# Two pairs' products with v in one TensorE run, token units of 256 and 320, and more pairs with v stationary, in a fused attention and two-MLP kernel

## The chip, the core and the metric

The kernel runs on one core of one Trainium2 chip. The metric is the device time of one execution in microseconds, lower is better. TensorE (PE) does the matrix products, VectorE (DVE) and ScalarE (ACT) the element-wise work, GpSimd (POOL) the reductions over partitions, SyncE (SP) issues most of the transfers.

## What is computed

q, k and v have 4 batches, 8 heads, 576 positions, 64 features, in float32. Heads 0 to 3 attend to the last 32 positions (plain), heads 4 to 7 to every fourth of the last 128 (dilated). The 2304 tokens of 512 features that come out go through two MLPs.

```python
scores = np.where(mask, scale * q @ k.T, -1e9)
attn = exp(scores - max) / (sum + 1e-9)
x = (attn @ v) -> (2304, 512)
y = leaky_relu(x @ w_in1, 0.01) @ w_out1       # d_ff 2048
out = softplus(y @ w_in2) @ w_out2             # d_ff 2048
```

## The kernel before

**Phase 1** is attention and the first MLP, interleaved on TensorE. Each float32 operand of the MLP is split into a high and a low part, and a product is three matmuls: high by high, high by low, low by high. The tokens go in units of `widths` = 256, 256, 352, 288, 288, 288, 288, 288 (line 448; the first two share one weight pass and are one unit of 512). A unit is 16 steps, one for each 128 rows of d_ff. A step has a group of 12 matmuls with w_in (`first_product`, line 833) and, two steps later, one of 12 with w_out (`g2`, line 876), each with the unit's tokens as the moving columns. Between them ScalarE makes the leaky ReLU and the high part, VectorE the low part (line 858). Each group's matmul is 128 by 128 by the unit's width.

**Attention** goes in 8 windows of 288 tokens (w = 0 to 7), each of four pairs of heads (p = 0, 1 plain, p = 2, 3 dilated). A pair's steps are: load q, k, v (lines 542, 552, 559), transposes on VectorE (603, 608, 614), scores on TensorE (674 plain, 661 dilated), mask (682, 689), the maximum over partitions on GpSimd (699), subtraction (703), exponent on ScalarE (706), and the product with v. The pairs of w = 0 and 1 are made early, before the first MLP group. There are two forms of what follows the exponent:

- The older form: the exponentials are stationary (`pv`, line 724), the sum comes as a 65th column of v, ScalarE and VectorE divide (734, 740, 741), and TensorE transposes the result (`xT`, line 750).
- The "turned" form keeps v stationary: `pv_late` (line 760) writes the result already transposed, in 12 matmuls of 96 columns for a plain pair and 16 of 72 for a dilated one; GpSimd sums the exponentials (768), VectorE spreads the sums (776), makes the reciprocals (781, 783, 784) and multiplies (788). A pair is turned from w = 3 on, but for p = 1 of w = 3 (line 495).

The result is split into the high part (`x_hi`, 807) and the low part (`x_lo`, 811) in the room of its unit; two rooms, for even and odd units, take turns. Since units 2 to 6 are windows 3 to 7 exactly, each such unit needs one window.

**Phase 2** is the second MLP: w_in2 by a seven-product scheme (line 1017; 1078 for the first 256 tokens), then w_out2 (line 1090).

**The order.** A planner inside the kernel (`run_schedule`) writes the order of every engine's instructions. Each `Op` has an engine, an assumed cost, dependencies, buffer slots that it takes (`acq`) and frees (`rel`), and a due time worked back from `target`, the planned time of the group that needs it. Slots that matter here: `at` (two PSUM banks for scores and products), `s` (two score tiles), `mx` (one tile for maxima and sums), `xn` (two result tiles), and two tiles of v. The TensorE order is fixed for the MLP groups, and the attention's matmuls are put between groups; engines then run their own queues in order. The planner knows that VectorE is slowed while GpSimd reduces. A product with v is planned at least `SLACKT` = 2.0 us after what it waits for, and a pair's low part 11 us (`STAG`) ahead of the next pair's, the fourth's due as its unit begins.

```python
pv = a.o_pv = Op("pe", 0.84, a.pv_late, deps=x + [lv],
                 order=[prev(1, "o_pv")], acq=["at", "xn"], **ms)
sm = Op("pool", 3.6, a.sums, deps=x, acq=[tag_mx], lib="reduce", **m)
t = Op("dve", 2 * dve(288), a.spread, deps=[sm, pv], rel=[tag_mx, tag_s], lock=LOCKT, **m)
t = Op("dve", 0.9, a.recip, deps=[t], acq=["rd"], rel=["rd"], lock=LOCKT, **m)
xt = Op("dve", dve(288, True), a.norm, deps=[t], rel=["at"], hold=HOLDS, **m)
```

Of the kernel before, what the change touches and what calls it, by code (L numbers as in the profile page):

```python
# [11 lines left out]
F32 = mybir.dt.float32  # L12
# [14 lines left out]
def kernel(  # L27
# [18 lines left out]
    nc = tc.nc  # L46
# [8 lines left out]
    TG = 384  # L55
# [30 lines left out]
    TURN = 3  # L86
# [7 lines left out]
    class Op:  # L94
        def __init__(self, eng, cost, fn, *args, deps=(), order=(), acq=(), rel=(),
                     target=None, margin=0.0, start=0.0, lib=None, slack=0.0, lock=0.0, optional=False, hold=0.0, lead=None, shy=False):
# [11 lines left out]
    def run_schedule(slots):  # L108
# [64 lines left out]
        running = {}  # L173

        def slowed(start, work, rate):
            beside = locked - start
            return start + (work / rate if work <= rate * beside else beside + work - rate * beside)

# [5 lines left out]
        while True:  # L184
# [17 lines left out]
            for e in engines:  # L202
# [3 lines left out]
                for o in pools[e]:  # L206
                    if ready_at[o] <= now + 1e-9 and all(free[a] >= o.acq.count(a) for a in o.acq):
                        rank = (ready_at[o] if e == "bw" else o.prio) + (HOLD if switch(o) else 0.0) + (WAIT if 0.0 < o.lock < 0.5 and now < locked else 0.0), o.n
                        if best is None or rank < best_rank:
                            best, best_rank = o, rank  # L210
# [24 lines left out]
                if best.lib == "reduce":  # L235
                    locked = best.end if now > LOCK_FROM else now + LOCKED
                    beside = running.get("dve")
                    if now > LOCK_FROM and beside is not None and beside.lock and beside.end > now:
                        beside.end = slowed(now, beside.end - now, beside.lock)
                        busy["dve"] = beside.end - TRAIL["dve"]  # L240
                        heapq.heappush(events, beside.end)
                        heapq.heappush(events, busy["dve"])
# [205 lines left out]
    widths = [256, 256, 352, 288, 288, 288, 288, 288]  # L448
# [22 lines left out]

    xparts, rows = {}, {}
# [12 lines left out]
    class Pair:  # L485
        def __init__(self, w, p):
# [8 lines left out]
            self.turned = w >= TURN and (self.dil or p == 0 or w > TURN)  # L495
# [276 lines left out]

# [17 lines left out]
        def x_views(self):  # L790

            w0 = self.w * T1
            for u in range(NUNIT):
# [3 lines left out]
                xh, xl = (t[:, self.p, lo - unit_at[u]:hi - unit_at[u]] for t in x_room(u))  # L797
# [5 lines left out]
                yield src, xh, xl  # L803

        def x_hi(self):
            for src, hi, _ in self.x_views():
                nc.scalar.activation(out=hi, in_=src, func=AF.Copy)

        def x_lo(self):
            for src, hi, lo in self.x_views():  # L810
                nc.vector.tensor_sub(out=lo, in0=src, in1=hi.bitcast(F32))  # L811
# [326 lines left out]
    NSPIN, LOCKED, LOCK, LOCK_FROM, SLACK0, SLACK, HOLDS = 150, 1.2, 0.33, 75.0, 0.3, 1.0, 1.5  # L1138
    LOCKT = 0.7
# [53 lines left out]
    for w in range(NW):  # L1193
        blocks = [b for b, (t, n) in enumerate(BLOCKS) if t < (w + 1) * T1 and t + n > w * T1]
        first_slot = min(slot(b) for b in blocks)
        rooms = sorted({unit_of[b] for b in blocks if BLOCKS[b][0] >= w * T1 and b != 1})
        for p in range(NPAIR):
# [58 lines left out]
            else:  # L1256
                nk = a.s0 + T1 - a.klo
                tk = Op("dve", dve(nk) if not dil or a.first else 2 * dve(nk), a.trans_k, deps=[lk] + old_kq, rel=["kr"], lock=LOCKT, **m)
                tq = [Op("dve", (1.0 if turned else 1.2) if dil else 0.48, a.trans_q, deps=[lq] + (old_kq if dil else []),
                         rel=["qr"] if dil else [], lock=LOCKT, **m)]  # L1260
# [25 lines left out]
            x = Op("dve", dve(576), a.less_max, deps=[r], rel=[tag_mx], lock=LOCK, **m)  # L1286
# [18 lines left out]
            room = [f"x{u % 2}" for u in rooms] if p == 0 else []  # L1305
            if not turned:
# [5 lines left out]
            xh = a.o_xh = Op("act", act(288, not turned), a.x_hi, deps=[xt], order=[prev(1, "o_xh")],  # L1312
                             acq=[] if not turned else room, **m)
            stag = STAG00 if w == 0 else STAG0 if w == 1 else STAG
            xl = Op("dve", dve(288, not turned), a.x_lo, deps=[xh], rel=[a.room(p)[1] if not turned else "xn"], lock=LOCK if turned else 0.0,
                    target=tau(first_slot) - 0.5 - stag * (NPAIR - 1 - p), **m)
            for b in blocks:
                xready.setdefault(b, []).append(xl)
            last_att.append(xl)
# [6 lines left out]
    for layer, f, which in pieces:  # L1326
# [20 lines left out]
        o = Op("dve", dve2(n), a.shift, deps=[o], acq=["cp"], lock=LOCK, **m)  # L1347
        o = Op("dve", dve(n), a.join, deps=[o], rel=["cp"], lock=LOCK, **m)
        o = Op("dve", dve(n), a.add, deps=[o, lw], rel=["raw"] if layer else [], lock=LOCK, **m)
        if layer == 0:  # L1350
            o = Op("act", act(n), a.split_hi, deps=[o], **m)
            wready[0, f] = Op("dve", dve(n), a.split_lo, deps=[o], rel=["cf"], lock=LOCK, **m)
# [276 lines left out]
```

## Time and profile before

| what | us |
|---|---|
| three runs, median (lowest to highest) | 892.06 (892.01 to 892.25) |
| the profiled execution, its own time | 890.93 |
| its span, first to last instruction | 889.1 |
| TensorE busy in the span | 878.9 |
| VectorE, ScalarE, GpSimd busy | 654.1, 399.1, 146.8 |

In the timelines of the trace a row is a run of equal instructions on one engine: start in us from the span's start, length, engine and line, what it writes and reads, the shape, and how many. Matmuls are pipelined: a row's length has the tail of its last matmul in it, so the pace is read from the distance of starts. When a timeline is asked for from a moment within a run, the run's row holds the matmuls that are left from there.

### The profile page before, as it was taken

The page shows a single profiled execution, that of the slowest core. Times are in us where ns is not written, and L with a number is a line of the kernel's source. Part 1 is how long each engine was busy: PE and PEld are TensorE (multiplying, and loading weights), DVE is VectorE, ACT ScalarE, POOL GpSimd, SP SyncE. Part 2 cuts the span into 40 slices and gives each one's busy share as a digit, 9 for nine tenths or more (in the row PEclk, how much of TensorE's full clock was granted, in tenths as well). Part 3 has the DMA queues.
Part 4 walks back from the last instruction along what each step waited for, and adds up shares of the span by engine and source line. Part 5 has one row for each costly group of instructions (what it writes and reads, how often), then busy time and mean ns, then how long its engine had stood idle before and what let it go on. Part 6 is the DMA issues. An engine that isn't in the chain of part 4 may idle for free.

```text
span 889.1 us, 16856 instructions
## 1 busy us (share of the span) xinstructions
PE 878.9 (99%) x6621; PEld 822.2 (92%) x6621; DVE 654.1 (74%) x1166; ACT 399.1 (45%) x780; POOL 146.8 (17%) x71
## 2 busy tenths in 40 slices
PE   9989999999999999999999999999999999999998
PEld 6889999999999999999999999989888898888886
DVE  5999986897897887978944766857765775576553
ACT  5878765345444443444445644324322432243231
POOL 6500120332452433435400000000000000000000
PEclk9999999999999999999999999999999999999999
DMA  9887235664644626435259578333533443334332
GB/s 236 240 261 261 49 83 190 173 180 144 168 123 135 167 65 181 99 107 153 77 167 304 149 227 252 116 101 114 163 122 97 142 146 109 102 112 149 95 95 96
DMA packets 150736, 132.19 MB, mean 149 GB/s; under 512 B 92480, under 2 KB 131200, under 8 KB 150656
## 3 DMA queue, kind: packets, MB, share of 16 engines
q1 hardware_dynamic: 149632, 129.96, 49.1%
q10 hardware_dynamic: 1024, 1.15, 0.5%
q8 instruction: 52, 0.85, 0.4%
q14 instruction: 28, 0.23, 0.1%
HBM read 104.86 MB, written 26.21 MB: 147 GB/s over the span
## 4 chain that ended last, share of the span: by engine, by line
PE 94%; DMA 2%; DVE 2%; ACT 1%; issue 1%; SPq 0%; DVEq 0%; ACTq 0%
PE yp L876 23%; PE yo L1090 23%; PE h L833 23%; PE h L1017 18%; PE hp L1078 3%; DMA raw<-in_moe_w_out_dram 2%; PE pv L760 1%; PE sc L661 1%; PE sc L674 1%; PE pv L724 1%; DVE cf L330 0%; DVE w L381 0%; PE xt L750 0%; DVE cf L339 0%; DVE xn L741 0%
## 5 line engine op out<-in xcount | busy, mean ns | idle before, releaser
L876 PE MATMUL yp<-gh,w 128*128 128x288 f32 (+2 forms) x1024 | 229.1, 299 | 0.0
L833 PE MATMUL h<-xh,w 128*128 128x288 f32 (+2 forms) x1024 | 226.7, 297 | 0.0
L1090 PE MATMUL yo<-wo,w 128*128 128x512 f32 x864 | 222.8, 395 | 0.0
L1017 PEld LDWEIGHTS h<-tr,w 128*128 128x128 f32 x1344 | 174.3, 188 | 11.1
L1090 PEld LDWEIGHTS yo<-wo,w 128*128 128x128 f32 x864 | 152.5, 188 | 27.1
L1017 PE MATMUL h<-tr,w 128*128 128x256 f32 x1344 | 176.7, 279 | 0.0
L876 PEld LDWEIGHTS yp<-gh,w 128*128 128x128 f32 x1024 | 171.3, 188 | 1.9
L833 PEld LDWEIGHTS h<-xh,w 128*128 128x128 f32 x1024 | 171.1, 188 | 1.1
L833 PE MATMUL h<-xl,w 128*128 128x288 f32 (+2 forms) x512 | 151.2, 295 | 0.4 <-DVE xl L811 0.4
L876 PE MATMUL yp<-gl,w 128*128 128x288 f32 (+2 forms) x512 | 150.9, 295 | 0.0
L1055 ACT ACTIVATE ex<-ex 128x512 f32<-128x512 f32 x72 | 45.5, 632 | 159.9 <-DVE ex L1052 158.4
L849 ACT ACTIVATE hc<-h 128x288 f32<-128x288 f32 (+2 forms) x128 | 52.0, 406 | 118.2 <-PE h L833 112.5
L833 PEld LDWEIGHTS h<-xl,w 128*128 128x128 f32 x512 | 96.2, 188 | 0.9 <-DVE xl L811 0.9
L876 PEld LDWEIGHTS yp<-gl,w 128*128 128x128 f32 x512 | 96.2, 188 | 0.1
L858 DVE TENSOR_TENSOR gl<-hc,gh 128x288 fp32r<-128x288 f32 (+2 forms) x128 | 73.9, 578 | 28.7 <-ACT gh L854 27.8
L699 POOL PARTITION_ALL_REDUCE mx<-s x24 | 50.0, 2083 | 243.1 <-DVE s L682 186.8
L768 POOL PARTITION_ALL_REDUCE sm<-s x19 | 71.1, 3740 | 31.8 <-ACT s L706 27.5
L1058 DVE SCALAR_TENSOR_TENSOR ex<-hs,ex 128x512 f32<-128x512 f32 x64 | 44.3, 692 | 35.9 <-ACT ex L1055 35.6
L1063 ACT ACTIVATE w<-ex 128x512 fp32r<-128x512 f32 x72 | 45.3, 629 | 32.8 <-DVE ex L1058 32.8
L321 ACT ACTIVATE cf<-raw 128x512 f32<-128x512 f32 (+1 forms) x48 | 39.9, 830 | 40.7 <-DMA raw<-in_moe_w_out_dram 15.4
L854 ACT ACTIVATE gh<-hc 128x288 fp32r<-128x288 f32 (+2 forms) x128 | 56.6, 442 | 2.9
L1067 DVE TENSOR_TENSOR w<-ex,w 128x512 fp32r<-128x512 f32 x72 | 49.7, 691 | 10.9 <-ACT w L1063 6.2
(113 smaller groups left out, 966.6 us busy)
## 6 DMA issues: line engine op xcount, KB each, us to landing
wo<-w2o SPq DMA_DIRECT2D x80, 512.0 KB, 3.6
raw<-in_moe_w_in_dram SPq DMA_DIRECT2D x32, 512.0 KB, 6.5
raw<-in_moe_w_out_dram SPq DMA_DIRECT2D x32, 512.0 KB, 4.2
w2o<-cf SPq DMA_DIRECT2D x16, 512.0 KB, 3.1
w2a<-cf SPq DMA_DIRECT2D x8, 512.0 KB, 2.6
w2s<-cs SPq DMA_DIRECT2D x8, 512.0 KB
w<-w2a SPq DMA_DIRECT2D x8, 512.0 KB
out_dram<-o SPq DMA_DIRECT2D x28, 128.0 KB, 3.0
```

The lines of the kernel that those rows point to most:

```text
L699: nc.gpsimd.partition_all_reduce(self.mx, self.sf, channels=P, reduce_op=bass_isa.ReduceOp.max)
L768: nc.gpsimd.partition_all_reduce(self.sm, self.sf, channels=P, reduce_op=bass_isa.ReduceOp.add)
L833: nc.tensor.matmul(out=h, lhsT=a[:, c, :], rhs=b_[:, c, :], start=(c == 0 and a is whi and b_ is xh), stop=(c == NC - 1 and a is wlo))
L849: nc.scalar.activation(out=hc, in_=hbank.pop(s), func=AF.Prelu, alpha=0.01)
L854: nc.scalar.activation(out=gh, in_=hcopy[s], func=AF.Copy)
L858: eng.tensor_sub(out=gl, in0=hcopy.pop(s), in1=gparts[s][0].bitcast(F32))
L876: nc.tensor.matmul(out=ybank[e][:, o:o + n], lhsT=a[:, e * P:(e + 1) * P], rhs=b_, start=(f == 0 and n == unit_len[u] and a is whi and b_ ...
L1017: nc.tensor.matmul(out=bank[m, b][:, half], lhsT=w[:, a, kb * P:(kb + 1) * P], rhs=t[:, b_, kb], start=(kb == 0 and a + b_ == 0), stop=(kb ...
L1055: nc.scalar.activation(out=self.ex, in_=self.ex, func=AF.Softplus)
L1063: nc.scalar.activation(out=self.gh, in_=self.ex, func=AF.Copy)
L1067: nc.vector.tensor_sub(out=self.gl, in0=self.ex, in1=self.gh.bitcast(F32))
L1090: nc.tensor.matmul(out=obank[c, t], lhsT=a, rhs=b_, start=(opens and n == 0), stop=(closes and n == 2))
```

## The change

1. Units: `widths` becomes 256, 256, 352, 288, 256, 320, 256, 320. Units 3 to 6 start at tokens 1152, 1408, 1728 and 1984. Windows 4 and 6 now reach 32 tokens into the next unit. Their results for these tokens go to a small tile (`x_held`), and when the next unit's room is free one ScalarE and one VectorE instruction (128 columns) split them into it. `TG`, the width of the step tiles, goes from 384 to 352.
2. The products with v of two pairs (p = 0 and 1, or 2 and 3) become one operation, `pv_two`, that waits for the reciprocals of both; it takes both `at` banks and frees both `s` tiles. Sums and reciprocals no longer wait for the product; `xn` is taken by `spread`.
3. `TURN` goes from 3 to 2: turned are now also p = 2 and 3 of w = 2 and p = 1 of w = 3.
4. The planner's picture of VectorE beside GpSimd becomes simpler: an operation marked `lock` that starts beside a reduction ends its own cost after a fixed time from the reduction's start (1.2 us, or 2.45 for a sum); the transposes carry no mark.

```diff
-    TG = 384
+    TG = 352
-    TURN = 3
+    TURN = 2
...
                 if best.lib == "reduce":
-                    locked = best.end if now > LOCK_FROM else now + LOCKED
...
+                    locked = now + (LOCKED if best.cost < 3.0 else LOCKEDS)
                 if best.lock and now < locked:
-                    best.end = slowed(now, best.cost, best.lock) if now > LOCK_FROM else locked + best.cost
-                running[e] = best
+                    best.end = locked + best.cost
...
-    widths = [256, 256, 352, 288, 288, 288, 288, 288]
+    widths = [256, 256, 352, 288, 256, 320, 256, 320]
...
+    split_unit = {
+        w: u for w in range(NEARLY, NW) for u in range(NUNIT) if w * T1 < unit_at[u] < w * T1 + T1}
+    HELD = T1 - widths[-2]
+    x_held = attp.tile([P, NC, HELD], F32, tag="hold", name="hold") if split_unit else None
...
-            self.turned = w >= TURN and (self.dil or p == 0 or w > TURN)
+            self.turned = w >= TURN and (self.dil or w > TURN)
...
         def pv_late(self):
             m, kn = self.m, self.kn
-            self.xn = att.tile([P, T1], F32, tag="xn", name="xn")
...
         def spread(self):
-
+            self.xn = att.tile([P, T1], F32, tag="xn", name="xn")
...
+    def pv_two(a, b):
+        a.pv_late()
+        b.pv_late()
+
+    def hold_hi(w):
+        u = split_unit[w]
+        nc.scalar.activation(out=x_room(u)[0][:, :, 0:HELD], in_=x_held, func=AF.Copy)
+
+    def hold_low(w):
+        xh, xl = (t[:, :, 0:HELD] for t in x_room(split_unit[w]))
+        nc.vector.tensor_sub(out=xl, in0=x_held, in1=xh.bitcast(F32))
...
-                pv = a.o_pv = Op("pe", 0.84, a.pv_late, deps=x + [lv],
-                                 order=[prev(1, "o_pv")], acq=["at", "xn"], **ms)
                 sm = Op("pool", 3.6, a.sums, deps=x, acq=[tag_mx], lib="reduce", **m)
-                t = Op("dve", 2 * dve(288), a.spread, deps=[sm, pv], rel=[tag_mx, tag_s], lock=LOCKT, **m)
-                t = Op("dve", 0.9, a.recip, deps=[t], acq=["rd"], rel=["rd"], lock=LOCKT, **m)
-                xt = Op("dve", dve(288, True), a.norm, deps=[t], rel=["at"], hold=HOLDS, **m)
+                t = Op("dve", 2 * dve(288), a.spread, deps=[sm], acq=["xn"], rel=[tag_mx], **m)
+                t = Op("dve", 0.9, a.recip, deps=[t], acq=["rd"], rel=["rd"], lock=True, **m)
+                a.late, a.lands, xt = t, lv, None
+                if p % 2:
+                    b_ = pairs[-1]
+                    a.o_pv = b_.o_pv = Op("pe", 2 * 0.84 - 0.3, pv_two, b_, a, deps=[t, b_.late, lv, b_.lands],
+                                          order=[pairs[-2].o_pv], acq=["at", "at"], rel=[tag_s, tag_s], **ms)
+                    xt = [Op("dve", dve(288, True), c_.norm, deps=[a.o_pv], rel=["at"], hold=HOLDS, **m) for c_ in (b_, a)]
...
+                if c_.p == NPAIR - 1 and w in split_unit:
+                    u = split_unit[w]
+                    held_op = Op("act", act(NC * HELD), hold_hi, w, deps=[b_.o_xh for b_ in pairs[-NPAIR + 1:]] + [xh],
+                                 acq=[f"x{u % 2}"], **m)
+                    held_lo = Op("dve", dve(NC * HELD), hold_low, w, deps=[held_op], target=tau(slot(u + 1)) - 1.0, **m)
+                    xready.setdefault(u + 1, []).append(held_lo)
```

## Rows read from the trace of the kernel before

**Rows 1.** The page: busy time by engine, and the group of GpSimd's sums.

```profile
PE 878.9 (99%) x6621; PEld 822.2 (92%) x6621; DVE 654.1 (74%) x1166; ACT 399.1 (45%) x780; POOL 146.8 (17%) x71
...
L768 POOL PARTITION_ALL_REDUCE sm<-s x19 | 71.1, 3740 | 31.8 <-ACT s L706 27.5 <-DVE xn L776 2.4 <-DVE s L703 1.9
```

**Rows 2.** Busy time by stretch: stretch, length, engines, granted clock, DMA share, GB/s.

```profile
39.20:57.00 17.80, 14.61 (x129) 12.93 (x128) 17.15 (x35) 12.76 (x28) 2.30 (x1) 1.00 0.66 159
57.00:146.20 89.20, 89.20 (x793) 88.58 (x792) 80.14 (x129) 62.08 (x110) 9.27 (x4) 1.00 0.54 160
146.20:449.80 303.60, 303.60 (x2406) 295.74 (x2404) 254.30 (x458) 135.18 (x281) 111.79 (x39) 1.00 0.50 140
449.80:885.00 435.20, 435.05 (x2809) 395.46 (x2807) 274.92 (x501) 159.83 (x301) 0.00 (x0) 1.00 0.45 142
```

**Rows 3.** The chain that ended last: whole groups of 12 at 256, 352, 288 columns.

```profile
62.25 1.40 PE yp L876 x12
...
163.52 1.92 PE yp L876 x12
...
453.03 1.60 PE h L833 x12
```

**Rows 4.** Timeline of PE, 321.8 to 324.2: a dilated pair's product, whole and in part.

```profile
321.77 0.29 PE L876 MATMUL yp<-gh,w 128*128 128x288 f32 x1
321.99 0.72 PE L760 MATMUL pv<-s,v 104*64 104x72 f32 x16
...
322.88 0.30 PE L833 MATMUL h<-xl,w 128*128 128x288 f32 x1
...
322.11 0.61 PE L760 MATMUL pv<-s,v 104*64 104x72 f32 x14
...
322.36 0.36 PE L760 MATMUL pv<-s,v 104*64 104x72 f32 x6
```

**Rows 5.** Timeline of PE, 285.6 to 288.2: a plain pair's product.

```profile
285.82 0.29 PE L833 MATMUL h<-xh,w 128*128 128x288 f32 x1
286.04 0.72 PE L760 MATMUL pv<-s,v 128*64 128x96 f32 x12
...
286.92 0.29 PE L876 MATMUL yp<-gl,w 128*128 128x288 f32 x1
```

**Rows 6.** Timeline of PE, 119.1 to 126.9: the older form, window 2, dilated.

```profile
119.72 0.28 PE L876 MATMUL yp<-gh,w 128*128 128x256 f32 x1
119.83 1.20 PE L724 MATMUL pv<-v,s 104*72 104x65 f32 x16
...
121.04 0.28 PE L833 MATMUL h<-xl,w 128*128 128x256 f32 x1
...
126.03 0.28 PE L833 MATMUL h<-xh,w 128*128 128x256 f32 x1
126.15 0.41 PE L750 MATMUL xt<-ident,xn 72*128 72x72 f32 x4
...
126.57 0.28 PE L876 MATMUL yp<-gl,w 128*128 128x256 f32 x1
```

**Rows 7.** Timelines of PE, POOL and DVE, 351.7 to 373: two pairs of window 6.

```profile
351.92 0.91 PE L674 MATMUL sc<-qr,kt 64*128 64x96 f32 x12
...
366.13 3.75 POOL L768 PARTITION_ALL_REDUCE sm<-s  x1 [1.19 <-DVE xn L776]
...
366.35 2.50 DVE L781 TENSOR_SCALAR rd<-xn 128x9 f32<-128x9 f32 x1
...
372.27 0.48 DVE L784 STREAM_TRANSPOSE xn<-rd 128x288 f32<-128x288 f32 x1
```

**Rows 8.** Timelines of DVE and PE where unit 3 begins, 272 to 275.

```profile
272.65 0.70 DVE L811 TENSOR_TENSOR xl<-xn,xh 128x288 fp32r<-128x288 f32 x1 [0.24 <-ACT xh L807]
...
273.69 0.29 PE L833 MATMUL h<-xh,w 128*128 128x288 f32 x1
```

**Rows 9.** Waits of the SP queue: who waited for whom, total us, times, longest.

```profile
SPq L559 <- PE pv L760: 27.9, 7, 7.8
```

More of the change, by code (lines that the diff above doesn't have):

```diff
@@ L95, in __init__ @@
         def __init__(self, eng, cost, fn, *args, deps=(), order=(), acq=(), rel=(),
-                     target=None, margin=0.0, start=0.0, lib=None, slack=0.0, lock=0.0, optional=False, hold=0.0, lead=None, shy=False):
+                     target=None, margin=0.0, start=0.0, lib=None, slack=0.0, lock=False, optional=False, hold=0.0, lead=None, shy=False):
             self.eng, self.cost, self.fn, self.args = eng, cost, fn, args
@@ L171, in begins @@
                 coming[u.eng].append(u)
[L173 to L177, printed above, removed]
         result = []
@@ L207, in run_schedule @@
                     if ready_at[o] <= now + 1e-9 and all(free[a] >= o.acq.count(a) for a in o.acq):
[L208 removed]
+                        rank = (ready_at[o] if e == "bw" else o.prio) + (HOLD if switch(o) else 0.0) + (WAIT if o.lock and now < locked else 0.0), o.n
                         if best is None or rank < best_rank:
@@ L796, in x_views @@
                     continue
-                xh, xl = (t[:, self.p, lo - unit_at[u]:hi - unit_at[u]] for t in x_room(u))
+                held = split_unit.get(self.w) == u
+                if held:
+                    xh = xl = x_held[:, self.p, 0:hi - lo]
+                else:
+                    xh, xl = (t[:, self.p, lo - unit_at[u]:hi - unit_at[u]] for t in x_room(u))
                 if self.dil:
@@ L802, in x_views @@
                     src = self.xp.rearrange("p i m -> p (i m)")[:, lo - w0:hi - w0]
-                yield src, xh, xl
+                yield src, xh, xl, held
         def x_hi(self):
-            for src, hi, _ in self.x_views():
+            for src, hi, _, held in self.x_views():
                 nc.scalar.activation(out=hi, in_=src, func=AF.Copy)
         def x_lo(self):
-            for src, hi, lo in self.x_views():
-                nc.vector.tensor_sub(out=lo, in0=src, in1=hi.bitcast(F32))
+            for src, hi, lo, held in self.x_views():
+                if not held:
+                    nc.vector.tensor_sub(out=lo, in0=src, in1=hi.bitcast(F32))
+    def pv_two(a, b):
[7 more added lines that the diff above has]
+        nc.vector.tensor_sub(out=xl, in0=x_held, in1=xh.bitcast(F32))
     gparts = {}
@@ L1195 @@
         first_slot = min(slot(b) for b in blocks)
-        rooms = sorted({unit_of[b] for b in blocks if BLOCKS[b][0] >= w * T1 and b != 1})
+        rooms = sorted({unit_of[b] for b in blocks if BLOCKS[b][0] >= w * T1 and b != 1 and split_unit.get(w) != unit_of[b]})
         for p in range(NPAIR):
@@ L1304 @@
                                 rel=[a.room(half if dil else p)[1], "rd"], **m))
-            room = [f"x{u % 2}" for u in rooms] if p == 0 else []
+            rooms_x = [f"x{u % 2}" for u in rooms]
+            room = rooms_x if p == 0 else []
             if not turned:
@@ L1311 @@
                 a.o_xt = xt
[L1312 to L1319, printed above, removed]
+            for c_, xt_ in ([(a, xt)] if not turned else zip((pairs[-1], a), xt) if p % 2 else ()):
+                at_ = n - p + c_.p
+                xh = c_.o_xh = Op("act", act(288, not turned) + (0.2 if w in split_unit else 0.0), c_.x_hi, deps=[xt_], order=[pairs[at_ - 1].o_xh if at_ else None],
+                                 acq=[] if not turned or c_.p else rooms_x, **m)
+                stag = STAG00 if w == 0 else STAG0 if w == 1 else STAG
+                xl = Op("dve", dve(288, not turned), c_.x_lo, deps=[xh], rel=[c_.room(c_.p)[1] if not turned else "xn"], lock=turned,
+                        target=tau(first_slot) - 0.5 - stag * (NPAIR - 1 - c_.p), **m)
+                for b in blocks:
+                    xready.setdefault(b, []).append(xl)
+                if c_.p == 0 and w - 1 in split_unit:
+                    xh.order.append(held_op)
+                if c_.p == 0 and w - 2 in split_unit:
+                    xh.order.append(held_lo)
+                if c_.p == NPAIR - 1 and w in split_unit:
[4 more added lines that the diff above has]
+                    xready.setdefault(u + 1, []).append(held_lo)
+                last_att.append(xl)
             pairs.append(a)
```

29 lines of the change are left out of this document (11 added, 18 removed).

## The prediction

> **What bounds the kernel now.** I read the page first: TensorE is busy 99% of the span [rows 1]. Busy time of pipelined matmuls overlaps, so I then asked by stretch [rows 2]. From 57.0 us to 449.8 us TensorE is busy for the whole of each stretch, and then for 435.05 of 435.20 us; the granted clock is 1.00 throughout, the 2.4 GHz level. The only idle time is before 57 us (14.61 busy of 17.80 us in the last stretch) and in the 4.1 us after the last matmul. No other engine is full: VectorE, the nearest, has 254.3 of 303.6 us in the main attention stretch. So this kernel is a start, a solid line of matmuls, and a short end. After 57 us a microsecond of TensorE work removed is one of the total, as long as nothing that TensorE waits for becomes late.
>
> **What a group costs.** The chain gives whole groups of 12 matmuls with no idle time: 1.40 us at 256 columns, 1.60 at 288, 1.92 at 352 [rows 3]. That is 116.7, 133.3 and 160.0 ns a matmul; the columns alone at 2.4 GHz are 106.7, 120.0 and 146.7, so what lies on top is 10.0, 13.3 and 13.3 ns.
>
> **The units.** Two pairs of units go from 288 + 288 to 256 + 320. Each unit has 32 groups (16 steps, two groups), so 64 pairs of groups change. 320 columns do not occur before. It lies midway between 288 and 352, which gives 1.76 us; that is the value I take. The change is 2 x 1.60 - 1.40 - 1.76 = 0.04 us for a pair of groups, and 64 x 0.04 = 2.6 us. Bounds: in proportion from 256 it is 1.75 (gain 3.2 us); along the step from 256 to 288 it is 1.80 (gain 0). The nearest rows are the two neighbours, so the midpoint.
>
> A page of the Trainium skill speaks against this term. TensorE: Matmul & The Clock Gate, Part 1 ("Wait — 56ns, not 53.3ns?"), says that a warm matmul takes its columns at 2.4 GHz plus a fixed 2.5 ns or so, whatever its width. By that rule 256 + 320 costs what 288 + 288 does and the sum loses this term. The rows disagree: 10.0 ns over at 256 and 13.3 at 288 [rows 3].
>
> **One run for two pairs.** A dilated pair's product costs 322.88 - 321.77 less two matmuls of 133 ns: 0.84 us [rows 4]. Within the run, eight matmuls go from 322.11 (14 left) to 322.36 (6 left), 31 ns each, so 16 are 0.50 us. The other 0.34 us are paid on entering and leaving: 0.22 us from the last MLP matmul to the first product where the pace is 0.13, slow first products, and again on the way back. A plain pair takes 286.92 - 285.82 - 0.27 = 0.83 us [rows 5], so I give it the same fixed part. Two pairs in one run pay it once. There are 19 turned pairs now (19 sums [rows 1]) and 22 after, so 11 runs, and 11 x 0.34 = 3.7 us. Bounds: nothing, if each pair pays it anyway, and 3.7.
>
> **Three more pairs with v stationary.** In the older form a dilated pair of window 2 costs 121.04 - 119.72 - 0.23 = 1.09 us for the product and 126.57 - 126.03 - 0.23 = 0.31 for the transpose [rows 6], 1.40 in all against 0.84: 0.56 us less. Two of them are 1.1 us; for the plain pair of window 3 I take 0.5, from the dilated one. Sum 1.6 us. For it GpSimd gets three more sums of 3.74 us [rows 1], and VectorE the longer chain of spreads and reciprocals; GpSimd is busy 9.3 of 89.2 us and 111.8 of 303.6 in the stretches that hold them [rows 2], so it has room.
>
> **What is added or moved at no cost.** The held tokens bring two windows x (four short copies, one ScalarE and one VectorE instruction of 128 columns), each well under the 0.70 us of a whole low part [rows 8]. They lie on ScalarE and VectorE ahead of a unit's start, beside TensorE's groups. If they were late, some 1 us for each of two units would stand bare. The narrower step tiles cost nothing. Transfers: the load of v for a later pair waits on the product that frees its tile, and the SP queue stands still for it (7 waits, 27.9 us, longest 7.8 [rows 9]). The first pair's tile is now freed later by two sums, spreads and reciprocals, some 10 us. Behind that wait stand later loads of q and k and of the second MLP's weights. None is used at once: the next two pairs start their scores only when the `s` tiles come free at the same joint product. The planner's simpler picture moves no work by itself, only the order; I put it at zero, within -1 and +2 us. The start is nearly the same list, so zero within 1 us.
>
> **Does the joint run come late?** The product now waits for POOL and VectorE, and every group behind it on TensorE would wait too. So I timed two neighbouring pairs. From the scores of the first at 351.92 to the end of the second's reciprocals at 372.75 it is 20.8 us, with a reciprocal step caught beside a sum (2.50 us) in it [rows 7]. With the planner's 2.0 us and a run of 1.3 us a block of two pairs holds the score tiles for 24.2 us. A window has two blocks, 48.4 us. A unit lasts 51 to 63 us: 32 groups of 1.40 or 1.76 us, four score runs of about 1 us each [rows 7] and two joint runs of 1.33. It fits, with a seventh to spare on the average of 57. Today's margin is thin by plan: the fourth pair of window 4 ends its low part at 273.35 and its unit begins at 273.69 [rows 8], without a stall. After the change pairs 2 and 3 end together, due 11 us earlier, so this moment gets safer.
>
> **The sum.** 2.6 + 3.7 + 1.6 = 7.9 us. The profiled execution goes from 890.93 to 883.0 (span 889.1 to 881.2). It stands 1.1 us under the median of the runs, so the median goes from 892.06 to 884.2.
>
> **Rivals.**
> - Units bring nothing: if the excess is one fixed amount and 320 costs 1.80, only 5.3 us go, and the time is 886.8. For it: two of the three widths have the same excess. Against it: 256 has less. 7%.
> - Merging brings nothing: if every product pays its way in because the second pair writes another bank, 4.2 us go, 887.9. Against it: within a run the 31 ns hold steady [rows 4]. 3%.
> - Part is lost again: VectorE is late by half a us or so at each of 11 joint runs, as it serves the reciprocals beside the sums [rows 7] and has a sixth of its time free [rows 2]. 11 x 0.5 = 5.5 us back, 889.7. 8%; a loss of about 8 us, no change, 5%.
> - Slower: the blocks do not fit. A block holds both score tiles, both banks and both result tiles, so no third pair starts meanwhile. VectorE's weight conversions could stretch a block. From 28.5 us on (half of 57) attention falls behind the MLP, and TensorE stands at each unit's first group. At 30 us it is 2 x 1.5 = 3 us for each of five windows, 15 us: 899.2. It decides the sign from 29.3 us on, where five windows lose 7.9. Against it: 24.2 us measured. 7%.
>
> **The numbers.** My forecast has 70%: 884.2 us. A measurement of this kernel can tell about 0.2% (1.8 us) from no change. The range takes the bounds of the units (0.6 us more gain, 2.6 less) and 1 us of the start; it reaches to the first two rivals, 882.5 to 888.0, together about 80%. Faster: 70 + 7 + 3 + 8 = 88%; same 5%; slower 7%.
>
> **What would show it.** Right: groups of 12 at 1.40 and near 1.76 us; 11 runs of 24 or 32 products that take about 1.33 us; three fewer older products and transposes in windows 2 and 3; TensorE busy for every whole stretch after 57 us; the last matmul about 8 us earlier. Wrong: waits of PE on the reciprocals' transpose, on a product's `s`, or on a unit's low parts; a group of 320 at 1.80; joint runs near 1.67 us; a start that ends later than 57 us.

## The result, and the profile after

The change is slower. Four runs have a median of 898.25 us (895.75 to 898.65) against 892.03 before; the ratio is 1.0066, 95% interval 1.0046 to 1.0087, which is 4 to 8 us. The profiled execution took 895.75 us (span 894.0, mean granted clock 0.998); the three others, 898.0 to 898.7, have 0.996, by an estimate from these clocks some 1.8 us more lost at the 1.2 GHz level. 884.2 was predicted. Three of the runs below, and the kernel before beside one of them, had one execution each some 13 to 15 us longer than its fellows, and the medians and ratios leave these out.

The page, beside [rows 1]:

```profile
PE 877.4 (98%) x6610; PEld 820.5 (92%) x6610; DVE 662.6 (74%) x1176; ACT 399.8 (45%) x785; POOL 160.1 (18%) x74
...
L758 POOL PARTITION_ALL_REDUCE sm<-s x22 | 83.8, 3811 | 41.3 <-ACT s L697 21.5
```

TensorE has 11 matmuls fewer, yet its busy time is only 1.5 us less and it is no longer busy throughout. Busy time by stretch, beside [rows 2] (length, then TensorE's matmuls, its weight loads, VectorE, ScalarE and GpSimd, each with its number of instructions, then the granted clock):

```profile
39.20:57.00 17.80, 14.41 (x127) 12.74 (x126) 17.04 (x35) 12.69 (x29) 1.80 (x1) 1.00 0.67 163
57.00:146.20 89.20, 88.22 (x780) 87.03 (x779) 84.18 (x128) 61.43 (x105) 17.57 (x6) 1.00 0.50 150
146.20:449.80 303.60, 298.02 (x2404) 290.47 (x2403) 254.48 (x462) 134.13 (x288) 116.80 (x40) 0.99 0.49 136
449.80:885.00 435.20, 435.18 (x2788) 396.64 (x2787) 277.74 (x507) 161.19 (x302) 0.00 (x0) 1.00 0.45 146
```

Before, TensorE was busy for the whole of the second and third stretch; now 1.0 and 5.6 us are missing, and VectorE has 84.2 of 89.2 us in the second where it had 80.1. In the third, where most of the loss is, VectorE is as busy as before: 254.5 us and 254.3. What TensorE waited for from 57 to 890 us (total, times, longest); for the kernel before the view shows no row there:

```profile
PE h L840 <- ACT xh L801: 2.2, 1, 2.2
PE yp L883 <- DVE gl L865: 1.8, 2, 1.6
PE yp L883 <- DVE ys L901: 1.1, 1, 1.1
PE xt L741 <- DVE s L673: 0.5, 1, 0.5
PE sc L652 <- DVE xl L806: 0.5, 1, 0.5
PE h L840 <- DVE xl L806: 0.3, 1, 0.3
```

That is 6.4 us, all on VectorE and ScalarE, none of it at a joint run. The largest stands at the start of unit 2. The timelines of ScalarE, VectorE and TensorE there (in brackets, how long the engine had stood idle and what released it):

```profile
212.08 0.67 ACT L308 ACTIVATE cf<-raw 128x512 f32<-128x512 f32 x1 [2.16 <-DMA raw<-in_moe_w_in_dram]
212.65 0.67 ACT L322 ACTIVATE raw<-raw 128x512 uint32<-128x512 uint32 x1
216.84 0.66 ACT L308 ACTIVATE cf<-raw 128x512 f32<-128x512 f32 x1 [3.52 <-DMA w2o<-cf]
217.41 1.29 ACT L801 ACTIVATE xh<-xn 128x288 fp32r<-128x288 f32 x2
...
212.78 0.43 DVE L313 TENSOR_SCALAR cp<-cf 128x512 uint32<-128x512 uint32 x1 [2.26 <-ACT cf L308]
213.12 0.81 DVE L778 TENSOR_TENSOR xn<-pv,xn 128x288 f32<-128x288 f32 x2
...
208.50 1.22 PE L750 MATMUL pv<-s,v 104*64 104x72 f32 x32
...
218.14 0.40 PE L840 MATMUL h<-xh,w 128*128 128x288 f32 x1 [2.25 <-ACT xh L801]
```

The chain through the same moment has one long piece (start, us, what):

```profile
210.11 6.63 DMA w2o<-cf
```

The results of window 3's last two pairs are multiplied out at 213.9, 4.2 us after their joint run ends, because VectorE's queue had a conversion ahead of them that waited for ScalarE and its raw weights. Their high parts need only ScalarE, but ScalarE's queue has a conversion of the second MLP's weights ahead of them, and that one stands for its buffer until a store that took 6.63 us has landed. TensorE waits 2.25 us for the high parts, whose inputs were ready 3.5 us before ScalarE began them. Right behind it, by the busy time of that stretch, the granted clock is 0.50, the 1.2 GHz level, which costs another 1.7 us:

```profile
218.90:222.30 3.40, 3.40 (x13) 3.40 (x14) 3.40 (x8) 1.49 (x4) 0.00 (x0) 0.50 0.46 147
```

**What TensorE has to do did fall.** The chain shows whole groups of 320 columns at 1.76 us, as forecast beside [rows 3], and the timeline a joint run, beside [rows 4]:

```profile
346.27 1.76 PE h L840 x12
348.03 1.77 PE yp L883 x12
```

```profile
388.05 0.30 PE L883 MATMUL yp<-gh,w 128*128 128x320 f32 x1
388.28 1.22 PE L750 MATMUL pv<-s,v 104*64 104x72 f32 x32
389.43 0.42 PE L840 MATMUL h<-xh,w 128*128 128x320 f32 x1
389.69 0.30 PE L840 MATMUL h<-xl,w 128*128 128x320 f32 x1
```

From 388.05 to 389.69, less two matmuls of 0.147, is 1.35 us for two pairs; 1.33 was forecast.

### The profile page after: what moved, and what is told of

Same layout as the page of the kernel before. It is cut to its first block, busy times and chain, and to the rows that moved or that the text cites. A ratio compares the mean times of both kernels' runs of the same rounds, so it can differ in the third digit from the quotient of the medians.

```text
span 894.0 us, 16840 instructions
## 1 busy us (share of the span) xinstructions
PE 877.4 (98%) x6610; PEld 820.5 (92%) x6610; DVE 662.6 (74%) x1176; ACT 399.8 (45%) x785; POOL 160.1 (18%) x74
## 4 chain that ended last, share of the span: by engine, by line
PE 80%; DVE 9%; DMA 5%; ACT 2%; issue 1%; POOL 1%; SPq 1%; DVEq 0%; ACTq 0%; POOLq 0%
PE yo L1097 23%; PE h L1024 18%; PE yp L883 17%; PE h L840 17%; DMA raw<-in_moe_w_out_dram 3%; PE hp L1085 3%; PE pv L750 1%; DVE cf L317 1%; PE sc L652 1%; DVE cf L326 1%; DVE gl L865 1%; DVE w L368 1%; DMA w2o<-cf 1%; DMA kr<-in_k_dram 1%; PE sc L665 1%
## 5 line engine op out<-in xcount | busy, mean ns | idle before, releaser
L883 PE MATMUL yp<-gh,w 128*128 128x256 f32 (+3 forms) x1024 | 229.1, 299 | 1.2 <-DVE ys L901 1.1
L840 PE MATMUL h<-xh,w 128*128 128x256 f32 (+3 forms) x1024 | 226.7, 297 | 2.2 <-ACT xh L801 2.2
L883 PE MATMUL yp<-gl,w 128*128 128x256 f32 (+3 forms) x512 | 152.0, 297 | 1.9 <-DVE gl L865 1.8
L840 PE MATMUL h<-xl,w 128*128 128x256 f32 (+3 forms) x512 | 151.3, 296 | 0.7 <-DVE xl L806 0.7
L856 ACT ACTIVATE hc<-h 128x256 f32<-128x256 f32 (+3 forms) x128 | 51.8, 405 | 109.1 <-PE h L840 89.4
L865 DVE TENSOR_TENSOR gl<-hc,gh 128x256 fp32r<-128x256 f32 (+3 forms) x128 | 76.8, 602 | 27.7 <-ACT gh L861 27.1
L758 POOL PARTITION_ALL_REDUCE sm<-s x22 | 83.8, 3811 | 41.3 <-ACT s L697 21.5
L308 ACT ACTIVATE cf<-raw 128x512 f32<-128x512 f32 (+1 forms) x48 | 40.1, 836 | 49.3 <-DMA raw<-in_moe_w_in_dram 15.6
L861 ACT ACTIVATE gh<-hc 128x256 fp32r<-128x256 f32 (+3 forms) x128 | 56.8, 444 | 3.3
```

The lines of the kernel that those rows point to most:

```text
L758: nc.gpsimd.partition_all_reduce(self.sm, self.sf, channels=P, reduce_op=bass_isa.ReduceOp.add)
L840: nc.tensor.matmul(out=h, lhsT=a[:, c, :], rhs=b_[:, c, :], start=(c == 0 and a is whi and b_ is xh), stop=(c == NC - 1 and a is wlo))
L856: nc.scalar.activation(out=hc, in_=hbank.pop(s), func=AF.Prelu, alpha=0.01)
L861: nc.scalar.activation(out=gh, in_=hcopy[s], func=AF.Copy)
L865: eng.tensor_sub(out=gl, in0=hcopy.pop(s), in1=gparts[s][0].bitcast(F32))
L883: nc.tensor.matmul(out=ybank[e][:, o:o + n], lhsT=a[:, e * P:(e + 1) * P], rhs=b_, start=(f == 0 and n == unit_len[u] and a is whi and b_ ...
```

## The experiments

Each run was timed beside the kernel before on the same chip. The chips differ from one group of runs to the next, so runs are compared with one another by their ratios. "Idle" is TensorE's stalls of over 0.15 us between 57 and 880 us, summed from the trace.

| run | median us | ratio to before (95%) | idle us |
|---|---|---|---|
| the change | 898.25 | 1.0066 (1.0046 to 1.0087) | 6.4 |
| no_joint | 897.92 | 1.0067 (1.0050 to 1.0085) | 4.3 |
| old_picture | 900.36 | 1.0096 (1.0081 to 1.0111) | 9.5 |
| picture_alone | 896.55 | 1.0055 (1.0038 to 1.0071) | 4.0 |
| due_19_us_earlier | 898.20 | 1.0079 (1.0062 to 1.0097) | 9.4 |
| control_1_us | 893.45 | 1.0012 (1.0002 to 1.0022) | 2.4 |
| units_alone | 892.87 | 1.0007 (0.9996 to 1.0018) | 2.8 |
| turn_alone | 894.22 | 1.0031 (1.0018 to 1.0044) | 2.6 |
| joint_alone | 895.92 | 1.0056 (1.0035 to 1.0077) | 6.0 |
| products_alone | 898.43 | 1.0068 (1.0052 to 1.0084) | 8.1 |
| window_2_undone | 898.54 | 1.0087 (1.0060 to 1.0114) | 6.7 |
| units_and_joint_old_picture | 899.58 | 1.0095 (1.0077 to 1.0113) | 7.9 |
| less_vector_work | 888.33 | 0.9956 (0.9940 to 0.9972) | 2.1 |
| light_loads | 889.64 | 0.9979 (0.9969 to 0.9988) | 2.8 |
| relieved_all | 888.21 | 0.9967 (0.9956 to 0.9979) | 2.8 |
| relieved_from_window_3 | 888.48 | 0.9972 (0.9961 to 0.9983) | 2.0 |
| relieved_joint | 888.59 | 0.9969 (0.9956 to 0.9982) | 1.0 |
| lighter_only | 888.97 | 0.9970 (0.9958 to 0.9983) | 2.3 |
| relieved_before | 890.06 | 0.9982 (0.9972 to 0.9991) | 0.0 |

### One part undone, one part alone, an earlier start

no_joint gives each pair its own product again, ahead of the spread:

```diff
+                pv = a.o_pv = Op("pe", 0.84, a.pv_late, deps=x + [lv], order=[prev(1, "o_pv")], acq=["at", "xn"], **ms)
...
-                t = Op("dve", 2 * dve(288), a.spread, deps=[sm], acq=["xn"], rel=[tag_mx], **m)
+                t = Op("dve", 2 * dve(288), a.spread, deps=[sm, pv], rel=[tag_mx, tag_s], **m)
```

> The change with part 2 undone: each pair has its own product with v again, behind its exponent; units, the three more pairs and the planner's new picture stay. Theory A (the joint run puts the product behind two sums and two reciprocals, which takes the lead that attention had over its unit): the stalls go and 11 x 0.34 = 3.7 us of TensorE work come back, 884.2 + 3.7 = 887.9 us, within 1.5. Rival B (the planner's simpler picture undercounts VectorE, so any order written with it comes late): the 6 us of waits and the slow clock stay, 896 us or more. Rival C (the units of 256 and 320 with held tokens cost it): as B, 896 or more.

old_picture takes part 4 out of the change, picture_alone puts it into the kernel before. The main lines, as old_picture has them (the `lock` marks change with them):

```diff
-                if best.lock and now < locked:
-                    best.end = locked + best.cost
+                if best.lock and now < locked:
+                    best.end = slowed(now, best.cost, best.lock) if now > LOCK_FROM else locked + best.cost
```

> The change with part 4 undone: the planner sees VectorE beside GpSimd as before, all else is changed. Theory A (joint run): the blocks of two pairs are as long as in the change, PE still waits at units, 893 to 899 us. Rival B (planner's picture): the order is kept again on the chip and most of the loss goes, 884 to 889 us. Rival C (units): 893 or more.

> The kernel before with part 4 alone: the planner's new picture, nothing else. Theory A (joint run) and rival C (units): 892.0 within 1 us, as a pair's product still follows its exponent and attention has a lead over its unit. Rival B (planner's picture): several us slower than before, 895 or more, with waits of PE on VectorE's low parts.

due_19_us_earlier has the attention due earlier in the plan:

```diff
-    MA, MC, MC1, MG, MY = 13.0, 0.0, 0.0, 3.0, 5.0
+    MA, MC, MC1, MG, MY = 32.0, 0.0, 0.0, 3.0, 5.0
```

> The whole change with one number altered: the planner's margin for attention steps is 32 us in place of 13, so a block of two pairs is begun some 19 us earlier. No work is added or left out. If the loss is attention that comes late to its unit (theory A, and rival B as far as it works through that): no wait of PE at a unit's first group, 884 to 887 us. If VectorE is short of time whatever is begun first: waits on the low parts of steps in place of those at units, 890 or more.

Undoing the joint run or the picture cures nothing: 897.9 and 900.4. That refutes theory A (no_joint was to come back to 887.9) and rival B as the one cause (old_picture was to fall to 884 to 889). Yet the picture alone costs 0.55%, 4.9 us, with the same matmuls as before; it alters nothing but the order, and B's number came, though the waits are mostly those of scores on VectorE's multiplications, not on low parts. An earlier start only moves the waits (3.0 us at 89 us for a transpose, 1.7 at 411). So there is no one guilty part, and what waits is not merely late for its unit.

### Is any order drawn anew slower? And each of the other parts

control_1_us is the kernel before with `MA` 14 instead of 13. units_alone has `widths` and the held tokens, turn_alone `TURN` at 2, joint_alone the joint runs from window 3 on, products_alone parts 2 and 3. window_2_undone is the change without window 2's turned pairs; units_and_joint_old_picture has the old picture as well. Of the lines that differ, that of units_alone and that of window_2_undone:

```diff
-    widths = [256, 256, 352, 288, 288, 288, 288, 288]
+    widths = [256, 256, 352, 288, 256, 320, 256, 320]
...
-            self.turned = w >= TURN and (self.dil or w > TURN)
+            self.turned = w > TURN
```

> The kernel before with one number of the planner changed: attention is due 14 us ahead of its use instead of 13. The work is the same, the planned end is the same to the nanosecond, only the order of the queues is drawn anew. Theory L (the order of before is a well-fitted one, and any list drawn anew loses several us on the chip because the planner's picture of waits and transfers is only rough): 894 to 899, with 2 to 5 us of TensorE waits after 57 us. Rival P (it is the parts of the change, through their own needs, that cost): 891.7 within 1 us and no waits after 57 us.

> The kernel before with part 1 alone (units of 256 and 320, held tokens, narrower step tiles; the old product operations, TURN 3 and the old picture). The matmuls are then 2.0 us shorter by the change's own rows (147 ns at 320 columns, 116.8 to 118 at 256, 133.5 at 288). Theory L: the order is drawn anew, 889.7 plus 2 to 5 us of waits: 891 to 895. Rival P, with the loss in the joint products or the picture: 889.5 within 1. Rival H (the held tokens, split only when the next unit's room is free, stand bare): TensorE waits on held low parts (the 128-column subtraction) at the starts of units 4 and 6, one us each, 891 to 892, and no other waits.

> The kernel before with parts 2 and 3 alone (joint products, TURN 2; old units, old picture). By the terms that the change's trace bore out it has 3.7 us of way into and out of products less and 1.6 us of older products less. Theory L: 886.5 plus 2 to 8 us of waits, 889 to 895. Theory B (blocks of two pairs take 31 to 34 us and hold both score tiles, both banks and VectorE's order, so attention falls behind the MLP): 892 to 900, with the waits of PE at unit starts (h on xh or xl) or on norms and steps that stand behind them. Rival P2 (the joint run is harmless and the loss is in the picture or the units): 886.5 within 1.

> The change, but the two dilated pairs of window 2 keep the older form (window 3 and later are turned, joint, with the new units and the new picture). TensorE's work is then some 5.9 us under the kernel before (units 2.0, ten joint runs 3.4, one older product 0.5): 886.0 if nothing waits. Theory W (the spreads and reciprocals of window 2's turned pairs fall into 57 to 146 us, where VectorE has 80 of 89 us taken, 84 to 85 with them; it falls behind there, and the lateness never goes away): no TensorE idle time before 146 us, 888 to 893. Rival B (blocks of two pairs are the trouble in every window): 894 to 898, with the waits between 200 and 450 us where they were. Rival L (any list drawn anew loses 1 to 3 us): 887 to 889, were W the rest.

> The same, with the old picture of VectorE beside GpSimd too: units, and joint products from window 3 on. 886.0 if nothing waits; the plan itself has 3.6 us of TensorE idle time in it at 325 and 347 us. Theory W plus the picture's cost of 5 us: this is the fastest of the variants, 887 to 891. Rival B: 894 to 898.

> The kernel before with joint products from window 3 on (and p = 1 of window 3 turned for that), old units, old picture, window 2 as before. Work 3.9 us under before: 888.0 if nothing waits. Theory W: 888 to 891. Rival B (the block of two pairs costs more than the way in and out that it saves): 893 to 898, as in the run with parts 2 and 3 together (898.4).

> The kernel before with TURN at 2 alone: three more turned pairs, separate products, old units, old picture. Work 1.6 us under before: 890.3 if nothing waits. Theory W: TensorE idle for 1 us or more between 57 and 146 us, VectorE's busy time there 84 to 85 us instead of 80, and 893 to 897 in all. Rival B: 890 to 892, and no idle time before 146 us.

One number of the planner, which only draws the order anew, costs 1.1 us (0.2 to 2.0) and brings 2.4 us of waits to a kernel that had none in its profile. The waits are what theory L said (2 to 5 us), the time lies between its 894 to 899 and rival P's 891.7; and picture_alone, a new order too, cost 4.9. So the order of before fits the chip better than both that were drawn in its place; how much of each part's cost is the loss of this good fit, and how much the part's own need, these runs do not separate.

The parts alone cost 0.6 (units, not told from zero), 2.8 (turn), 5.0 (joint) and 4.9 us (picture), 13.3 in sum, where all four together cost 5.9. But for the picture, each was expected to bring work less, and each brings waits instead. Theory W came in turn_alone's time and in VectorE's busy time from 57 to 146 us (84.93 us instead of 80.14), but not as the cause: the wait of 2.1 us stands at 206 us, and without window 2 the loss was as large. Rival B has the times of products_alone and joint_alone and nearly those of window_2_undone and units_and_joint_old_picture (both above its 898), but no_joint, without any block of two pairs, is as slow. joint_alone shows how a wait is made. GpSimd, VectorE and TensorE:

```profile
408.84 3.61 POOL L771 PARTITION_ALL_REDUCE sm<-s  x1 [1.60 <-ACT s L710]
...
408.91 3.02 DVE L339 CUSTOM_DVE_ANT_0 cf<-raw,cf 128x1024 uint16<-128x1024 uint16 x1
411.85 1.49 DVE L618 STREAM_TRANSPOSE qz<-qr 64x288 f32<-64x288 f32 x2
413.37 0.43 DVE L349 TENSOR_TENSOR cs<-cf 128x256 f32<-128x256 f32 x1
413.71 0.95 DVE L779 STREAM_TRANSPOSE xn<-sm 64x288 f32<-64x288 f32 x2
...
416.19 0.45 DVE L878 TENSOR_TENSOR gl<-hc,gh 128x288 fp32r<-128x288 f32 x1
...
416.70 0.40 PE L896 MATMUL yp<-gl,w 128*128 128x288 f32 x1 [2.48 <-DVE gl L878]
```

An addition of the weight conversion, 0.68 us in the median of its like, starts 0.07 us behind a sum and takes 3.02. Everything behind it on VectorE moves back, the transposes and the spread among them, and the MLP's low part (`gl`) comes at 416.19, 2.5 us too late for TensorE, which from 417.65 runs 3.4 us at the 1.2 GHz level (granted clock 0.50). The kernel before has an instruction held beside a sum as well (2.50 us in [rows 7]), and no wait of TensorE from it, so a hold alone does not make a wait.

### Is it VectorE's work, or standing still for transfers?

Both runs keep every queue of the change in its order. less_vector_work shortens two VectorE instructions (the join and the add) in each conversion of the second MLP's weights; light_loads moves a quarter of their raw bytes. Both leave work out and are for finding the cause only. The edits in part, first that of the add:

```diff
+            n = self.n // 8 if self.layer else self.n
-            nc.vector.tensor_tensor(out=self.cf, in0=self.cf, in1=self.raw[:, :, 0], op=ALU.add)
+            nc.vector.tensor_tensor(out=self.cf[:, :n], in0=self.cf[:, :n], in1=self.raw[:, :n, 0], op=ALU.add)
...
```

> The change with every queue in the same order, but two of VectorE's instructions in each conversion of the second MLP's weights (the join and the add) take an eighth of their columns: that leaves out part of the weights' low bits, and some 1.1 us of VectorE work in each of 32 conversions, 35 us in all, nearly all of it between 120 and 450 us. Theory V (VectorE runs behind its plan because its work takes longer than the planner thinks, and the lateness ends at TensorE): the waits after 57 us shrink to under 2 us, and the time falls to 890 to 893. Theory D (the queues stand still for transfers, raw weights in and split weights out, and what is queued behind them is late): the waits stay within 1.5 us of the change's 7, 896.5 to 898.5.

```diff
-                nc.sync.dma_start(out=raw, in_=src[f * P:(f + 1) * P, :])
+                n_ = 2 * P if self.layer else 2 * DM
+                nc.sync.dma_start(out=raw[:, :n_], in_=src[f * P:(f + 1) * P, :n_])
...
```

> The change with every queue in the same order and the same work on each engine, but each transfer of the second MLP's raw weights brings a quarter (128 KB instead of 512), which is converted four times over: three quarters of these weights are left out. Theory V (VectorE's own work decides): within 1.5 us of the change, 896.5 to 899. Theory D (the in-order queues stand still for the raw weights, and what stands behind is late; ScalarE waits 26 us for them in the change, VectorE another 12 behind ScalarE): 890 to 894, and TensorE's waits after 57 us fall from 6.4 us to under 3.

Both bring it back: 888.33 and 889.64, by the ratios 9.8 and 7.8 us better than the change, with the same matmuls. less_vector_work goes theory V's way and light_loads theory D's, each to below the range given and far from the other theory's; less_vector_work keeps 2.1 us of waits, not under 2, and took 28 us from VectorE (634.4 us busy instead of 662.6), not 35. TensorE's waits in less_vector_work:

```profile
PE yp L885 <- DVE gl L867: 0.9, 2, 0.7
PE xt L743 <- DVE s L675: 0.5, 1, 0.5
PE sc L654 <- DVE xl L808: 0.5, 1, 0.5
PE yp L885 <- ACT ys L901: 0.2, 1, 0.2
```

Its third stretch, where VectorE is busy 233.0 us instead of the change's 254.5:

```profile
146.20:449.80 303.60, 302.51 (x2464) 296.41 (x2464) 233.00 (x468) 137.69 (x296) 114.48 (x40) 1.00 0.50 140
```

The two theories are not rivals: with the order fixed, the queues lose their slack to instructions and to standing still alike, and either, taken away, gives it back. In light_loads VectorE is as busy as in the change (663.7 us by its page), so it is not the busy time alone that counts. Which transfers count the run does not tell, as fewer raw bytes relieve all of them (103 GB/s in the third stretch instead of 136).

### The change, relieved

Nothing is left out in these versions. The sum of a pair's exponentials is at least 1 (the largest is exp 0), so adding 1e-9 in float32 changes nothing; ScalarE copies all of y; and, but for lighter_only, the planner is told later landing times.

```diff
-            nc.vector.tensor_scalar_add(
-                out=rd, in0=self.xn.rearrange("p (b c) -> p b c", c=32)[:, :, 0], scalar1=1e-9)
-            nc.vector.reciprocal(out=rd, in_=rd)
+            nc.vector.reciprocal(out=rd, in_=self.xn.rearrange("p (b c) -> p b c", c=32)[:, :, 0])
...
-                    eng = "act" if e % 2 == 0 else "dve"
+                    eng = "act"
...
-    STORED = 2.0
+    RS, KS = 1.5, 1.0
+    STORED = 4.0
...
-        o = Op("act", act(n), a.rebias, deps=landed, acq=[] if layer and which == 0 and f % 2 else ["cf"], **m)
+        o = Op("act", act(n), a.rebias, deps=landed, slack=RS if layer else 0.0, acq=[] if layer and which == 0 and f % 2 else ["cf"], **m)
```

> The change in full, made lighter for VectorE without leaving anything out: the addition of 1e-9 to a sum that is at least 1 is dropped (in float32 it changes nothing; 22 held instructions of 0.2 to 1.1 us), VectorE's half of the copies of y goes to ScalarE (some 14 of 0.5 us), and the planner is told that raw weights land 1.5 us later, q and k 1.0 us later, and a store 2 us later. That is 12 to 20 us of the 35 that the run with less VectorE work took away. Theory V: half of its 9.9 us, 892 to 895. If the landing times were what hurt (D): 887 to 891. Rival (neither): 896 to 899.

> The same without the turned pairs of window 2. Work 3.6 us under the kernel before by the sizes measured so far (units 0.5, ten joint runs 2.6, one older product 0.5): 888.3 if nothing waits, and the plan has no idle time. V: 890 to 893. Rival: 896 to 899, as the same parts without the relief (898.5).

> The kernel before with joint products from window 3 on, old units and old picture, relieved in the same way. Work 3.1 us under: 888.8 if nothing waits. V: 889 to 892, against 895.9 without the relief. Rival: 894 to 897.

> The change with the lighter VectorE work (no addition of 1e-9, y copied by ScalarE), but with the planner's old landing times. Theory V (the work decides): 888 to 890.5, and ScalarE's waits for raw weights stay near 26 us. Theory D (the order, in which conversions stand in the queues before their weights have landed, decides): 893 to 898.

> The kernel before with the same relief (no addition of 1e-9, y copied by ScalarE, later landing times in the plan) and no part of the change. TensorE has no wait after 57 us to lose and no work less. If the parts of the change bring the 3 us: 891 to 893. If it is the relief alone: 888 to 889.

All three relieved variants and lighter_only beat both kernels, by about 3 us against before and, by the ratios, about 9 against the change; among themselves they can't be told apart. All three relieved variants lie below the ranges that theory V gave. The page of relieved_all:

```profile
PE 874.5 (99%) x6610; PEld 819.2 (92%) x6610; DVE 647.3 (73%) x1140; ACT 403.1 (45%) x799; POOL 158.7 (18%) x74
```

And what its TensorE waits for from 57 to 890 us:

```profile
PE sc L652 <- DVE xn L776: 1.1, 1, 1.1
PE yp L881 <- DVE gl L863: 0.7, 1, 0.7
PE xt L741 <- DVE s L673: 0.5, 1, 0.5
PE sc L652 <- DVE xl L804: 0.5, 1, 0.5
```

15 us of VectorE work less were worth some 9, more than the half that was expected; 888.2 is in the range given for the landing times (D), so relieved_all alone does not say which half of the relief did it. lighter_only does: with the old landing times it is at 888.97, in V's range. The other half of that forecast missed: ScalarE's waits for raw weights did not stay near 26 us (15.6 and 10.6 in the change, 57 to 450 us) but grew:

```profile
ACT cf L308 <- DMA raw<-in_moe_w_out_dram: 20.9, 11, 4.7
ACT cf L308 <- DMA raw<-in_moe_w_in_dram: 16.9, 7, 4.8
```

So these waits did no harm once VectorE had slack. The planner sees the lighter work, so unlike the two runs before, these versions have orders of their own; that four of them come out alike speaks against a lucky one. relieved_before missed both of its forecasts: with no part of the change it is 0.18% faster than before, 1.6 us, though the profiled execution of before shows no wait to remove (its other executions reach 892.7). Where these 1.6 us come from is not shown: in the two profiles the first MLP takes the same time within 0.1 us. The relief and the parts thus share the 3 us, 0.18 and 0.15 of 0.33%, each known to about 0.1%; in the profiles the span is 888.3 for relieved_before and 886.4 for relieved_all.

## Why the prediction was wrong

**The work on TensorE** was forecast in the main rightly. By the traces of before and of relieved_all, the first MLP group to the last is 470.4 and 468.1 us, and 2.8 of the latter are idle: 5.1 us of work went, where the terms had 7.9.
- Joint runs: right, 11 x 0.34.
- Turned pairs: right within 0.2; three older products and their transposes against three of 0.84.
- Units: 1.5 us, not 2.6. The 320-column matmul takes 147 ns as forecast, but the 256-column one in units 3 and 5 takes 118.1 on the mean, not the 116.7 of [rows 3]: 768 x (2 x 133.5 - 118.1 - 147.0) ns. The rule of the Trainium skill (TensorE: Matmul & The Clock Gate, Part 1) of 2.5 ns over the columns would, by an estimate, make 135.8 of the 147; the trace still speaks against it.
- Not foreseen: the 256-column matmul of the first unit takes 117.4 instead of 116.8 ns, 0.5 us in sum, and the runs of scores are about 1.0 us longer in sum (a plain pair's costs TensorE 1.07 us instead of 1.04, ways in and out included). What lengthens them was not settled.

**The step that failed** is the section on what is "added or moved at no cost", in its sentence "The planner's simpler picture moves no work by itself, only the order; I put it at zero, within -1 and +2 us". In its place stand 6.4 us of waits and 1.7 us at the 1.2 GHz level. picture_alone, an order and nothing else, measures 4.9 us, interval 3.4 to 6.3; even one number of the planner costs 1.1. It is not part 4 as such, since the change with the old picture is no faster: each part draws the order anew, and no order drawn without relief kept TensorE free of waits.

**The step that failed with it** is the reading of VectorE. For "the longer chain of spreads and reciprocals" the forecast gave no price and no reason, and checked the room on GpSimd alone; VectorE's "sixth of its time free" [rows 2] stood only in a rival of 8%. From 57 to 146 us VectorE had 9 us free before and has 5 after. From 146 to 450 us it is equally busy, without a wait of TensorE in one order and with 5.6 us missing in the other: the busy share counts neither the time that VectorE stands in its queue nor how soon a result is needed. That its work matters is shown with the order fixed (less_vector_work), and some 15 us of it less, in new orders, are worth about 9 us of the kernel.

**"It fits"** was right on the size that it worked out, and left a piece out. The time that a block holds the score tiles, from its first scores to the end of its joint run, was put at 24.2 us from [rows 7]; in the change's ten blocks from window 3 on it is 23.1 to 31.9 us, 25.7 on the mean. But the next block begins its scores only 27.6 to 35.2 us after the last one began, 29.7 on the mean, mostly because a bank comes free only when VectorE has multiplied the product out, up to 4.2 us after the joint run. The rival let attention fall behind from 28.5 us on; by its rule 29.7 us would cost 2 x 1.2 us in each of five windows, 12 in all. TensorE did stand at a unit's first group, but once, for 2.5 us. So its condition came and its consequence did not: a block also stretches over the time that the plan leaves it. "This moment gets safer" held where it was said (window 4's last low part ends at 277.93, its unit begins at 280.48: 2.6 us ahead, where it had been 0.3) and failed one unit earlier, where the pair that is split at 217 to 219 belongs to a unit that begins at 214.8.

**The rival that was nearest** is "part is lost again: VectorE is late", put at 5.5 us and 8%. Right in the engine for the most part, wrong in the place: no wait stands at a joint run, whose products have their reciprocals in time; the waits are those of a unit's high parts, behind a store on ScalarE, and of the MLP's own low parts, copies and scores in VectorE's queue. Of the signs that were to show the forecast wrong one came, a wait on a unit's low parts (0.3 us), and of those that were to show it right the solid TensorE after 57 us did not.

The account of the profiled executions, which differ by 4.8 us: from the first MLP group to the last the change takes 5.4 us more, 6.7 of waits (short ones and those before 57 us too), 1.7 at the 1.2 GHz level and 1.4 in slower matmuls right behind the waits, less 4.4 of work. The other 0.6 is gained outside.

## What to carry to other kernels

Where one engine is full and its helpers work through their queues in order, price every edit on the helpers first, its order included: here each of four parts alone, however little work it moved, brought late results that cost what it saved or more, and 15 us of VectorE work less turned the same change from 6 us slower to 3 us faster. A busy share says nothing of slack; look for who stands behind whom in an in-order queue, and test with the order fixed and the helper's work cut. Time a mere redraw of the order as a control, before a loss is put down to a part. Compare a winning variant with the old kernel given the same relief, as about half of the gain here was the relief's.

## What was unexpected of the hardware

- A VectorE instruction that starts just behind a GpSimd sum takes 3.02 us instead of 0.68 (joint_alone), but it ends 0.5 us before the sum does (411.93 and 412.45). The Trainium skill (SBUF — State Buffer, "SBUF: two separate sides") says that the loser of the shared port blocks for the whole instruction of the other. By the rows, whose times for GpSimd are rough, it was released after some 2.4 us of 3.61 (an estimate: its end less its usual length).
- A wait of 2.25 us costs more than itself: the next 3.4 us ran at the 1.2 GHz level (granted clock 0.50), 1.7 us lost. The wait of 1.6 us at 324 us had no such stretch behind it, nor had one of 2.29 us in window_2_undone (to 323.6 us).
- One 512 KB store took 6.63 us beside six loads of v, where its like took 3.1 in the median before, 3.5 at most. What lengthened it is not shown.
